# Some full matrix products of an attention-and-convolution kernel issued as one 128-column matmul instead of two 64-column ones

## The chip, the core and the metric

The kernel runs on one core of a Trainium2 chip. The time is device microseconds of one execution; a kernel's time is the median of several. Before the change it is 215.59 us, the median of three runs (215.33, 215.59 and 215.70).

The core's engines run side by side and meet at semaphores: TensorE (PE in the profile, with its weight loads shown apart as PEld), VectorE (DVE), ScalarE (ACT), GpSimd (POOL) and SyncE (SP). PE multiplies into PSUM, and ACT and DVE take the results out of it.

## The reference

Eight sequences of 576 steps with 8 heads of width 64. Linear attention without a softmax, a norm per head, and then a gated long convolution:

```python
kv  = einsum('bhsd,bhse->bhde', k, v)
out = einsum('bhsd,bhde->bhse', q, kv)
x   = out / sqrt(mean(out*out, -1) + 1e-6) * g_norm      # -> (8, 576, 512)
proj = x @ w_proj                                        # 512 -> 3 * 512
x1, x2, x3 = proj[..., :512], proj[..., 512:1024], proj[..., 1024:]
x2_conv = irfft(rfft(x2, axis=1) * rfft(filter_fft, axis=0))
out = (x1 * x2_conv * x3) @ w_out
```

## The kernel before

**The order of the work is written by hand.** The string `ORDER` at the top lists some 700 words such as `Ga1.2`: a step and the sequence that it works on. The loop at the end of the kernel runs through the words and calls each step's function, so every engine gets its instructions in exactly this order. Nothing is moved by a scheduler.

**The steps that run on PE**, and what each reads:

- `K` (L374): `kv` of one sequence, 48 small matmuls of 64 moving columns, for pairs of heads side by side. `T0`, `T1` (L412): 12 PE transposes each, of q. For sequences 3 to 7 the step `Qt` has SP issue a DMA transpose of q instead (L399).
- `O01`, `O23` (L451): q times kv, in 64x64 pieces. `R0` to `R3` (L462, or L464 through `mm2`): the sum of squares of a head, by a product with the matrix of ones `ind`.
- `Ga0` to `Ga3`, `Gb0` to `Gb3` (L637): the projections x1 and x3, 8 full products of 288 columns each; `GaP`, `GaQ`, `GbP`, `GbQ` are parts of the last of them. `rrM`, `rrT`, `abM`, `abT`: the projection x2, folded for the transform.
- `F0`, `F1`, `F2` and the remainders `F1t`, `F2t`: the forward transform as products with tables. `I01`, `Io01`, `I23`, `Io23` and the uncut forms `J..`: the inverse one. DVE and POOL multiply by the filter between them (`M..`, `A..`, tiles `tpw` and `Y`).
- `U0`, `U2`, `U4` and, for the last sequence, `V0` to `V3`: the product with `w_out`, of 512 columns.
- ACT and DVE evict: `eK` copies kv into `kvblk` (ACT, L380), `eTs` the transposed q (ACT, L416), `sq`, `ob`, `rs` and `x1..` are further ACT steps, `g..` is DVE's product of the two gates (L645), `M2` (L627) is DVE's product for `F2`.

**Three tilings of PE's array are in use.** A matmul of 128 rows and 64 weight columns uses half of the array, one of 64 rows and 64 columns a quarter, and a transpose the whole. The function `mm2` makes a full product of 128 weight columns out of two half-array matmuls, the first on columns 0 to 63 and the second on 64 to 127, with the same moving data:

```python
for c in (0, 64):
    nc.tensor.matmul(out[c:min(c + 64, m)], lhsT[:, c:min(c + 64, m)], rhs, start=start, stop=stop, tile_position=(0, c))
```

All the steps with full products call `mm2`: R, H (the filter's tables), rrM, abM, abT, F0, F1, Ga, Gb, I, J, U and V. `K`, `rrT`, `F2`, `Ff` and the idle products of `W` are in half tiles by their nature, `O`, `F1t` and `F2t` in quarter tiles, `T` and `Tb` in full ones. 2,989 matmuls run on PE in all; 1,117 full products by `mm2` are 2,234 of them.

PSUM is four tiles of two banks (`ps`), which `take` and `free` hand round: a step on PE waits until the eviction of the step that had the tile before is done.

Of the kernel before, what the change touches and what calls it, by code (L numbers as in the profile page):

```python
# [19 lines left out]
ORDER = """Lf.0 Zi.0 Z.0 W.3.2 Zt.0 An.0 W.0.12 Act.0 Zg.0 Gc.0 W.1.3 Zd.0 Zf.0 Tb1.0 Lvb.0 Lkb.0 Zz.0 Ff2.0 Ff1.0 Tb0.0 Lqb.0  # L20
# [37 lines left out]
def kernel(  # L58
# [11 lines left out]
    nc = tc.nc  # L70
# [25 lines left out]
    def take(key, n=2):  # L96
        i = min((x for x in range(4) if seen[x] is not None), key=lambda x: seen[x])
        held[key], seen[i] = i, None
        t = pair[i] if n == 2 else pair[i][:, 0]
        for _ in range(tmp.pop("idle", 0)):  # L100
            mm2(pair[i][:, 0], ind, kvblk[1].rearrange("p a b c -> p (a b c)"), start=True, stop=True)
        return t
# [5 lines left out]
    def mm2(out, lhsT, rhs, start, stop):  # L108
        mode[0] = 128
        m = lhsT.shape[-1]  # L110
        for c in (0, 64):
            nc.tensor.matmul(out[c:min(c + 64, m)], lhsT[:, c:min(c + 64, m)], rhs, start=start, stop=stop, tile_position=(0, c))  # L112

    made = {}
    mode = [128]

    def buf(name, i, shape, dt=BF16, tag=None, bufs=1):
        if (name, i) not in made:
            made[name, i] = work.tile(shape, dt, name=name, tag=tag or "%s%d" % (name, i), bufs=bufs)
        return made[name, i]  # L120
# [206 lines left out]
    def gen_h(g):  # L327
        ff = tmp['ff']
        hp = take("h")
        n = N1 if g == 0 else P  # L330
        for ri in range(2):
            for a in range(3):
                mm2(hp[:n, ri], FW[:, a, 2 * g + ri, 0:n], ff[:, a, ri], start=(a == 0), stop=(a == 2))
        u = work.tile([P, 2, DM], FP32, name="hu", tag="ot%d" % g)
        if g < 2:
            todo = [(HH[:n, g, 1], 0, cf[:n, 0, g:g + 1], cf[:n, 1, g:g + 1]),
                    (HH[:n, g, 0], 1, cf[:n, 0, g:g + 1], cf[:n, 2, g:g + 1])]
        else:
            todo = [(HM[:, i], 0, pc[:, 2 * i:2 * i + 1], pc[:, 2 * i + 1:2 * i + 2]) for i in range(2)]
        if g < 2:  # L340
            act.activation(out=u[:n], in_=hp[:n], func=AF.Copy, scale=todo[0][2])
        else:
            for i in range(2):
                act.activation(out=u[:n, i], in_=hp[:n, 0], func=AF.Copy, scale=todo[i][2])
        for i, (o_, ri, c1, c2) in enumerate(todo):
            vec.scalar_tensor_tensor(out=o_, in0=hp[:n, 1 - ri], scalar=c2, in1=u[:n, i], op0=ALU.mult, op1=ALU.add)  # L346
        free("h")
# [107 lines left out]
    def R(b, j):  # L455
        split = mode[0] == 64
        r2 = tmp['r', b, j] = take(("r", b, j))
        for h in range(2):
            x_ = sq()[:, j, h * TH:(h + 1) * TH]
            if split:  # L460
                for c in (lo, hi):
                    nc.tensor.matmul(r2[c, h, 0:TH], ind[c, c], x_[c], start=True, stop=True)  # L462
            else:
                mm2(r2[:, h, 0:TH], ind, x_, start=True, stop=True)  # L464
# [226 lines left out]
    full = [False]  # L691
# [142 lines left out]
            for e, q_ in (("s", nc.sync), ("g", nc.gpsimd), ("a", nc.scalar)):  # L834
                step["d%s%d%d" % (e, c, i)] = lambda b, c=c, i=i, q_=q_: o_dma(b, 1 + 2 * c, ot_tile(b, c // 2 * 2)[:, c % 2], (q_,), (i,))

    for word in ORDER.split():
        n, b, *idle = word.split(".")
        b, tmp["idle"] = int(b), int(idle[0]) if idle else 0
        clock[0] += 1  # L840
        step[n](b)
# [30 lines left out]
```

## Time and profile before

| | |
|---|---|
| time, median of 3 runs | 215.59 us (215.33 to 215.70) |
| profiled execution, its own time | 216.72 us |
| its span, from the first to the last instruction | 214.9 us |
| mean granted TensorE clock | 0.991 |
| PE busy | 201.8 us, 94% of the span, 2,989 matmuls |
| DVE busy | 174.9 us, 81% |
| ACT busy | 155.3 us, 72% |
| POOL busy | 59.3 us, 28% |

A row of the timeline view has the start of a group of instructions, the time until the last of them ends, the engine, the line, the operation with what it writes and reads, and the count; in brackets stands the idle time of the engine before it and who ended it. A matmul's row gives rows x weight columns, and after it the moving data. The time of one matmul contains its latency (a half-array matmul of 288 columns takes 291 ns in the mean), while the next can start long before it ends: how fast PE goes is read from start to start, not from the mean of one.

### The profile page before, as it was taken

The page shows a single profiled execution, that of the slowest core. Times are in us where ns is not written, and L with a number is a line of the kernel's source. Part 1 is how long each engine was busy: PE and PEld are TensorE (multiplying, and loading weights), DVE is VectorE, ACT ScalarE, POOL GpSimd, SP SyncE. Part 2 cuts the span into 40 slices and gives each one's busy share as a digit, 9 for nine tenths or more (in the row PEclk, how much of TensorE's full clock was granted, in tenths as well). Part 3 has the DMA queues.
Part 4 walks back from the last instruction along what each step waited for, and adds up shares of the span by engine and source line. Part 5 has one row for each costly group of instructions (what it writes and reads, how often), then busy time and mean ns, then how long its engine had stood idle before and what let it go on. Part 6 is the DMA issues. An engine that isn't in the chain of part 4 may idle for free.

```text
span 214.9 us, 6961 instructions
## 1 busy us (share of the span) xinstructions
PE 201.8 (94%) x2989; PEld 143.3 (67%) x2989; DVE 174.9 (81%) x242; ACT 155.3 (72%) x249; POOL 59.3 (28%) x88
## 2 busy tenths in 40 slices
PE   7998779999979999999999999999999999999990
PEld 6464468577858687677675868675676774697560
DVE  6565887599984999999979999798987999995650
ACT  3787777989787998897989985794865655426320
POOL 7970390036005900400063013003102100400752
PEclk9999978999999999999999999999999999999999
DMA  4999999999998999958849956231441244151573
GB/s 64 181 204 202 205 175 200 204 191 160 190 181 138 133 203 205 203 92 118 161 100 154 241 85 89 67 97 37 111 107 34 71 118 112 47 126 26 153 219 119
DMA packets 39938, 29.68 MB, mean 138 GB/s; under 512 B 14500, under 2 KB 35556, under 8 KB 39908
## 3 DMA queue, kind: packets, MB, share of 16 engines
q0 software_dynamic: 22080, 17.89, 53.6%
q1 hardware_dynamic: 17588, 11.02, 23.9%
q8 instruction: 23, 0.38, 0.8%
q10 hardware_dynamic: 240, 0.33, 0.5%
q14 instruction: 7, 0.06, 0.1%
HBM read 33.69 MB, written 9.44 MB: 201 GB/s over the span
## 4 chain that ended last, share of the span: by engine, by line
PE 83%; DMA 5%; POOL 3%; ACT 2%; DVE 2%; issue 2%; POOLq 0%; ACTq 0%; DVEq 0%
PE ps L112 73%; DMA vb<-in_v_dram 5%; PE ps L374 2%; PE ps L451 2%; PE ps L540 2%; PE ps L604 1%; PE ps L578 1%; PE ps L598 1%; DMA out_dram<-x 1%; DVE HM L346 1%; DVE HH L346 1%; POOL qb L129 1%; POOL kb L129 1%; PE ps L412 1%; ACT rstd L478 1%
## 5 line engine op out<-in xcount | busy, mean ns | idle before, releaser
L112 PE MATMUL ps<-x,wp 128*64 128x288 bf16 (+2 forms) x1024 | 73.0, 290 | 0.7 <-DVE x L492 0.6
L112 PEld LDWEIGHTS <-wp 128*64 128x64 bf16 x1024 | 59.3, 111 | 9.5 <-issue 2.7
L618 POOL TENSOR_TENSOR Y<-tpw 97x1024 bf16<-97x1024 f32 x8 | 18.9, 2364 | 109.5 <-DVE tpw L612 69.1
L612 DVE TENSOR_TENSOR tpw<-ps,HH 97x2048 f32<-97x2048 f32 (+1 forms) x16 | 36.6, 2287 | 1.8 <-PE ps L112 0.9
L112 PE MATMUL ps<-wo,yg 128*64 128x512 bf16 (+1 forms) x296 | 34.7, 374 | 0.0
L645 DVE TENSOR_TENSOR g<-ps,x 128x576 bf16<-128x576 f32 x30 | 22.5, 755 | 10.6 <-PE ps L112 9.4
L478 ACT ACTIVATE rstd<-ps,bias_eps 128x576 bf16<-128x576 f32 x32 | 23.0, 748 | 5.2 <-PE ps L112 3.8
L557 ACT CAST x<-ps 128x1024 bf16<-128x1024 f32 (+1 forms) x24 | 21.0, 879 | 7.7 <-PE ps L540 5.4
L112 PEld LDWEIGHTS <-yg 128*64 128x64 bf16 x296 | 16.3, 110 | 14.3 <-issue 1.8
L643 ACT CAST x<-ps 128x576 bf16<-128x576 f32 x30 | 19.5, 650 | 8.1 <-PE ps L112 7.8
L705 ACT CAST eo<-ps 128x576 bf16<-128x576 f32 x32 | 19.9, 658 | 6.3 <-PE ps L112 6.1
L112 PE MATMUL ps<-wp,ab 128*64 128x512 bf16 x192 | 23.3, 379 | 0.0
L467 ACT ACTIVATE sq<-ps 128x576 bf16<-128x576 f32 x32 | 20.4, 653 | 2.2 <-PE ps L451 2.0
L474 ACT ACTIVATE o<-ps,g_col 128x576 bf16<-128x576 f32 x28 | 20.6, 748 | 0.0
L112 PE MATMUL ps<-IV,Y 128*64 128x192 bf16 (+3 forms) x384 | 18.6, 239 | 1.5 <-issue 1.5
L112 PEld LDWEIGHTS <-Y 128*64 128x64 bf16 (+1 forms) x384 | 16.6, 110 | 3.4 <-issue 1.6
L788 ACT COPY ot<-ps 128x1024 f32<-128x1024 f32 x12 | 12.2, 1017 | 8.9 <-PE ps L112 8.8
L112 PEld LDWEIGHTS <-ind 128*64 128x64 bf16 x158 | 11.2, 119 | 8.5 <-DVE HH L346 1.8
L112 PEld LDWEIGHTS <-ab 128*64 128x64 bf16 x192 | 10.4, 110 | 7.7 <-issue 0.3
L492 DVE TENSOR_TENSOR x<-o,rstd 128x1152 bf16<-128x1152 bf16 x16 | 11.6, 752 | 4.7 <-ACT rstd L478 4.6
L112 PE MATMUL ps<-sq,ind 128*64 128x288 bf16 x116 | 11.0, 287 | 2.2 <-DVE HH L346 1.0
L627 DVE TENSOR_TENSOR Y<-ps,HM 128x1024 bf16<-128x1024 f32 x8 | 9.8, 1222 | 3.4 <-PE ps L604 3.1
(141 smaller groups left out, 288.7 us busy)
## 6 DMA issues: line engine op xcount, KB each, us to landing
out_dram<-ot SPq DMA_DIRECT2D x108, 64.0 KB, 1.7
vb<-in_v_dram POOLq DMA_DIRECT2D x7, 576.0 KB, 11.7
kb<-in_k_dram POOLq DMA_DIRECT2D x7, 576.0 KB, 10.7
qb<-in_q_dram POOLq DMA_DIRECT2D x7, 576.0 KB, 13.5
wp<-in_moe_w_proj_dram POOLq DMA_DIRECT2D x3, 512.0 KB, 15.5
fn<-in_moe_filter_fft_dram POOLq DMA_DIRECT2D x1, 576.0 KB, 6.5
vb<-in_v_dram POOLq DMA_DIRECT2D x2, 288.0 KB, 7.3
kb<-in_k_dram POOLq DMA_DIRECT2D x2, 288.0 KB, 6.8
```

The lines of the kernel that those rows point to most:

```text
L112: nc.tensor.matmul(out[c:min(c + 64, m)], lhsT[:, c:min(c + 64, m)], rhs, start=start, stop=stop, tile_position=(0, c))
L467: act.activation(out=halves(sq()[:, j]), in_=tmp['o', b, j][:, :, 0:TH], func=AF.Square)
L474: act.activation(out=by_time(osb(), j), in_=i_, func=AF.Copy, scale=g_col)
L478: act.activation(out=by_time(rstd(), j), in_=by_row(tmp['r', b, j]), func=AF.Abs_reciprocal_sqrt, scale=1.0 / D, bias=bias_eps)
L492: vec.tensor_mul(out=xt(b)[:, j0:j1], in0=osb()[:, j0:j1], in1=rstd()[:, j0:j1])
L557: act.copy(out=o_(), in_=tmp[key, b])
L612: vec.tensor_mul(out=t_[:n], in0=xp[:n].unsqueeze(1).to_broadcast([n, 2, 2, DM]), in1=two)
L618: op(out=Yt()[:n, 2 * g:2 * g + 2], in0=t_[:n, ::-1, 0], in1=t_[:n, ::-1, 1])
L643: act.copy(out=x1, in_=pp[:, :, 0:TH])
L645: vec.tensor_mul(out=halves(g13t(b)[:, dc]), in0=pp[:, :, 0:TH], in1=x1)
L705: act.copy(out=eo()[:, h, d0:d0 + 2], in_=tmp['i', b, d0, h][:, :, 0:TH])
L788: act.copy(out=ot, in_=tmp['u', b, c0])
```

## The change

`mm2` gets a second way: where the flag `wide[0]` is set it issues one matmul with all 128 weight columns in place of the two halves. The flag is set per word of `ORDER` by a small pass ahead of the kernel's body. The pass walks through the words, calls the tiling of each step "quarter", "half", "full" or "any" (a step made of `mm2` products can be either half or full), and collects runs of "any" steps. A run becomes full where neither neighbour is half, or where one neighbour is full; the other runs stay as they were. The order of the words is kept, and with it the order of the work on every other engine.

```diff
     def mm2(out, lhsT, rhs, start, stop):
         mode[0] = 128
         m = lhsT.shape[-1]
+        if wide[0]:
+            nc.tensor.matmul(out, lhsT, rhs, start=start, stop=stop)
+            return
         for c in (0, 64):
             nc.tensor.matmul(out[c:min(c + 64, m)], lhsT[:, c:min(c + 64, m)], rhs, start=start, stop=stop, tile_position=(0, c))
...
+    wide = [False]
+    words = ORDER.split()
+
+    def tile_of(n, last):
+        if n in ("O01", "O23", "F1t", "F2t") or n[0] == "R" and last == "quarter":
+            return "quarter"
+        if n in ("K", "Ka", "Kb", "rrT", "F2", "W") or n[:2] == "Ff":
+            return "half"
+        if n in ("T0", "T1", "Tb0", "Tb1", "Tb2", "Gc"):
+            return "full"
+        if n[0] in "RHIJUV" and n[1] != "N" or n[:2] in ("rr", "Ga", "Gb", "F0", "F1") or n in ("abM", "abT"):
+            return "any"
+        return None
+
+    runs, last = [], "half"
...
+    whole = set()
+    for a_, at, b_ in runs:
+        if (a_ != "half") + (b_ != "half") == 2 or "full" in (a_, b_):
+            whole.update(at)
...
-    for word in ORDER.split():
+    for i_, word in enumerate(words):
         n, b, *idle = word.split(".")
+        wide[0] = i_ in whole
```

Eleven runs with 334 of the 1,117 full products become full, and PE has 2,655 matmuls instead of 2,989. In the order of the program:

| run | products | before it | behind it |
|---|---|---|---|
| R0.0 | 2 | full (T1.1) | full (T0.1) |
| Ga1.0 Ga0.0 | 16 | quarter | quarter |
| R1.1 abM.0 | 10 | half (rrT.0) | full (T0.2) |
| F0.0 | 3 | full (T0.2) | full (T1.2) |
| Ga3.0 | 8 | full (T1.2) | half (K.2) |
| Gb2.0 F1.0 | 10 | quarter | quarter |
| Gb2.1 Ga0.2 F1.1 | 18 | quarter | quarter |
| Gb0.2 to F1.2 | 41 | quarter | quarter |
| U2.0 to Ga2.3 | 30 | quarter | quarter |
| Gb3.3 to abT.4 | 24 | quarter | quarter |
| U0.5 to the end | 172 | quarter (F1t.7) | the end |

PE's list, between the transposes of sequence 2 and the step F0.0 (tables FW and FX, 97 rows of result), before:

```order
L412 MATMUL ps_69<-ident,qb_74 128x96
L112 LDWEIGHTS FW
L112 MATMUL ps_68<-x_703,FW 64x512
L112 LDWEIGHTS FW
L112 MATMUL ps_68<-x_703,FW 33x512
L112 LDWEIGHTS FX
L112 MATMUL ps_68<-x_703,FX 64x512
L112 LDWEIGHTS FX
L112 MATMUL ps_68<-x_703,FX 33x512
```

And the same place now, down to the next transposes:

```order
L446 MATMUL ps_69<-ident,qb_74 128x96
L112 LDWEIGHTS FW
L112 MATMUL ps_68<-x_685,FW 97x512
L112 LDWEIGHTS FX
L112 MATMUL ps_68<-x_685,FX 97x512
L112 LDWEIGHTS FX
L112 MATMUL ps_68<-x_685,FX 97x512
L446 LDWEIGHTS qb_74
L446 MATMUL ps_67<-ident,qb_74 128x96
```

Six matmuls have become three, and the array's tiling no longer changes on the way from the transposes into F0.0 and back. Counted over the whole list, the tiling changes 60 times where it changed 64 times: twice less around F0.0 and twice less around R0.0. At R1.1 and Ga3.0 a change of tiling moves from one end of the run to the other.

The second place is row 1,717 of PE's list, in the step Io01.0 (products of Y with the table IV, 192 and 96 columns), before, with the row in the middle of these:

```order
L112 LDWEIGHTS Y
L112 MATMUL ps_66<-IV,Y 64x192
L112 LDWEIGHTS Y
L112 MATMUL ps_66<-IV,Y 64x96
L112 LDWEIGHTS Y
L112 MATMUL ps_66<-IV,Y 64x96
L112 LDWEIGHTS wp
```

Row 1,717 of the list now, again in the middle, lies in the step I01.0, which comes three steps later:

```order
L115 LDWEIGHTS Y
L115 MATMUL ps_66<-IV,Y 64x192
L115 LDWEIGHTS Y
L115 MATMUL ps_66<-IV,Y 64x192
L115 LDWEIGHTS Y
L115 MATMUL ps_66<-IV,Y 64x96
L115 LDWEIGHTS Y
```

Ahead of it 49 products have become full, so 98 rows (49 weight loads and 49 matmuls) are gone from the list, and every later instruction stands 98 rows further forward.

The third place is the start of the last run, where the quarter-tile step F1t.7 hands over to U0.5 (tiles yg and wo), before:

```order
L578 LDWEIGHTS FZ
L578 MATMUL ps_66<-x_703,FZ 64x512
L112 LDWEIGHTS yg
L112 MATMUL ps_69<-wo,yg 64x512
L112 LDWEIGHTS yg
```

And now:

```order
L612 LDWEIGHTS FZ
L612 MATMUL ps_66<-x_685,FZ 64x512
L112 LDWEIGHTS yg
L112 MATMUL ps_69<-wo,yg 128x512
L112 LDWEIGHTS yg
```

The tiling still changes once here, from quarter to full instead of from quarter to half, and from here to the end all products are full ones.

More of the change, by code (lines that the diff above doesn't have):

```diff
@@ L115 @@
     mode = [128]
+    wide = [False]
[12 more added lines that the diff above has]
+    for i_, word in enumerate(words):
+        n_ = word.split(".")[0]
+        k_ = tile_of(n_, last)
+        if k_ is None:
+            continue
+        if k_ == "any":
+            if last != "any":
+                runs.append([last, [], "quarter"])
+            runs[-1][1].append(i_)
+        elif last == "any":
+            runs[-1][2] = k_
+        last = k_
+    whole = set()
+    for a_, at, b_ in runs:
+        if (a_ != "half") + (b_ != "half") == 2 or "full" in (a_, b_):
+            whole.update(at)
     def buf(name, i, shape, dt=BF16, tag=None, bufs=1):
@@ L835 @@
                 step["d%s%d%d" % (e, c, i)] = lambda b, c=c, i=i, q_=q_: o_dma(b, 1 + 2 * c, ot_tile(b, c // 2 * 2)[:, c % 2], (q_,), (i,))
-    for word in ORDER.split():
+    for i_, word in enumerate(words):
         n, b, *idle = word.split(".")
+        wide[0] = i_ in whole
         b, tmp["idle"] = int(b), int(idle[0]) if idle else 0
```

## The prediction

> **What bounds the kernel.** First the page: the span, the busy shares, the chain that ended last, and the queue that brings PE its instructions.
>
> ```profile
> span 214.9 us, 6961 instructions
> PE 201.8 (94%) x2989; PEld 143.3 (67%) x2989; DVE 174.9 (81%) x242; ACT 155.3 (72%) x249; POOL 59.3 (28%) x88
> PE 83%; DMA 5%; POOL 3%; ACT 2%; DVE 2%; issue 2%; POOLq 0%; ACTq 0%; DVEq 0%
> q8 instruction: 23, 0.38, 0.8%
> ```
>
> PE is the bound: 83% of the chain are its matmuls. So the question is what a full product costs PE in each form. In the timeline of a steady stretch, four gates of 8 products of 288 columns, all as half-tile pairs:
>
> ```profile
> 186.08 4.09 PE L112 MATMUL ps<-x,wp 128*64 128x288 bf16 x64
> 190.00 1.16 PE L112 MATMUL ps<-IV,Y 128*64 128x288 bf16 x16
> ```
>
> 32 pairs take 190.00 - 186.08 = 3.92 us, 122.5 ns each, 0.425 ns per column. The two halves of a pair run side by side, and their weight loads cost nothing to be seen. **A full product can gain only where this stream is interrupted.** The interruptions are in the timeline around F0.0 (transposes at L412, then F0.0, transposes, Ga3.0, K.2); two grouped rows, one of PE and one of its loads, give the duration of one transpose and of its load.
>
> ```profile
> 41.73 0.38 PE L112 MATMUL ps<-wp,ab 128*64 128x512 bf16 x2
> 42.05 0.68 PE L412 MATMUL ps<-ident,qb 96*128 96x96 bf16 x12
> 42.66 0.40 PE L112 MATMUL ps<-x,FW 96*64 96x512 bf16 x2
> 42.89 0.60 PE L112 MATMUL ps<-x,FX 128*33 128x512 bf16 x4
> 43.43 0.69 PE L412 MATMUL ps<-ident,qb 96*128 96x96 bf16 x12
> 44.05 1.17 PE L112 MATMUL ps<-x,wp 128*64 128x288 bf16 x16
> 45.05 0.32 PE L374 MATMUL ps<-vb,kb 96*64 96x64 bf16 x10
> ```
>
> ```profile
> L412 PE MATMUL ps<-ident,qb 96*128 96x96 bf16 x72 | 4.1, 207 | 0.0
> L412 PEld LDWEIGHTS <-qb 96*128 96x128 bf16 x72 | 3.3, 98 | 1.1 <-issue 1.0
> ```
>
> The 12 transposes last 0.68 us and the last one 0.207, so they start (0.68 - 0.207)/11 = 43 ns apart. The last starts at 42.52, and F0.0 follows 0.14 later: the change of tiling costs 0.14 - 0.04 = 0.10 us. At 42.05 it is the same (0.32 after the last 512-column pair, which takes 0.22 at 0.425 ns per column), at 43.43 (last pair at 42.89 + 0.22 = 43.11, 0.32 again) and at 44.05 (0.14). **Each change of tiling costs PE 0.10 us, whichever two tilings.** Ga3.0 then takes 45.05 - 44.05 = 1.00 us for 8 pairs where 0.98 would do: 0.02 more for the first pair behind a change.
>
> **The steady cost of a full product.** No plain full-array product is in the trace; the nearest rows are the transposes, which are full-array matmuls with a load of 128 new weight columns each. They start 43 ns apart at 96 columns, where 0.425 x 96 is 41. So the load hides under only 41 ns of streaming, and 120 ns or more should cover it better. Bounds: 0 to 2 ns per product, up to 334 x 2 = 0.7 us in all; I take 0, since 288 columns give three times the cover. Below 0 it can't go, because the pairs already run at the column rate.
>
> The Trainium skill, "TensorE: Matmul & The Clock Gate", under "What overlaps and what doesn't", says that a weight load overlaps running matmuls only when the row groups differ. It speaks against the change, as all row groups of a full product are the same. The transposes disagree: a load of 98 ns in the mean sits in steps of 43. By the rule the loads of full products would be exposed; that is a rival below.
>
> **Changes of tiling.** There are four fewer. Two are at R0.0, in this piece of the timeline:
>
> ```profile
> 28.01 0.44 PE L112 MATMUL ps<-sq,ind 128*64 128x288 bf16 x4 [0.73 <-DVE HM L346]
> 28.38 0.68 PE L412 MATMUL ps<-ident,qb 96*128 96x96 bf16 x12
> 29.26 0.76 DVE L492 TENSOR_TENSOR x<-o,rstd 128x1152 bf16<-128x1152 bf16 x1 [0.64 <-ACT rstd L478]
> 30.07 0.64 PE L112 MATMUL ps<-x,wp 128*64 128x288 bf16 x3 [0.64 <-DVE x L492]
> ```
>
> R0.0 waits for DVE anyway, which hides the change ahead of it. The one behind it only brings T0.1 forward, and the next step that decides, Ga1.0 at 30.07, waits for DVE's x. R0.0's second product may come 0.01 sooner. I count 0 for both.
>
> The other two are around F0.0 and stand on PE's path: 2 x 0.10, and 0.02 for its second pair. At R1.1 and abM.0 one change moves ahead of the run: R1.1 starts 0.10 later, abM.0 ends where it did. At Ga3.0 one moves behind it, for another 0.02. So K.2 starts about 0.25 us sooner. Not all of it goes on; here are ACT's timeline and the step O01.2 behind K.2's eviction (`kvblk`):
>
> ```profile
> 41.07 2.10 ACT L557 CAST x<-ps 128x1024 bf16<-128x1024 f32 x2
> 43.07 2.20 ACT L416 COPY qT<-ps 128x1152 bf16<-128x1152 bf16 x2
> 45.26 0.64 ACT L643 CAST x<-ps 128x576 bf16<-128x576 f32 x1
> 46.02 1.14 ACT L380 CAST kvblk<-ps 128x256 bf16<-128x256 f32 x3
> ```
>
> ```profile
> 47.21 0.44 PE L451 MATMUL ps<-qT,kvblk 64*64 64x288 bf16 x8
> ```
>
> ACT works without a gap from 41.07 to 45.90, is free for 0.12, and evicts K.2 until 47.16; O01.2 starts 0.05 behind that. So about 0.12 can go through. Bounds: 0.02 (if the 0.10 that R1.1 loses delays ACT's row as well) and 0.25; I take **0.15**.
>
> **The instruction stall.** PE's largest single gap after 31 us waits for no semaphore. The timeline, and PE's matmuls counted up to three points:
>
> ```profile
> 61.55 0.55 PE L112 MATMUL ps<-IV,Y 128*64 128x192 bf16 x10
> 63.58 0.23 PE L112 MATMUL ps<-IV,Y 97*64 97x96 bf16 x2 [1.48 <-issue]
> 63.62 0.81 PE L112 MATMUL ps<-x,wp 128*64 128x288 bf16 x10
> ```
>
> ```profile
> 0.00:57.90 57.90, 52.13 (x727) 0.97 1.18 179
> 0.00:61.90 61.90, 56.13 (x859) 0.97 1.18 180
> ```
>
> It stops in the middle of Io01.0, ten matmuls in, 1.64 us behind the time that the two left would have started (61.94). My reading: PE ran out of instructions. Queue q8 moved 23 packets, and PE had 2 x 2,989 = 5,978 loads and matmuls, 260 to a packet. Between 57.9 and 61.9 PE used 2 x (859 - 727) = 264 of them, a whole packet in 4.0 us, where the mean is 214.9/23 = 9.3, since K.4 and K.3 pack 48 matmuls into 0.76 us each. The DMA view of 61.0 to 62.3 has one such packet, on engines that are full of loads:
>
> ```profile
> q8 instruction: 1, 0.02, 4.9%
> ```
>
> Now 98 instructions ahead of this point are gone, so the packet's edges move 98 rows on. One falls from 57.9 (start of K.4) to about 59.3, in abM.1. The other falls from row 1,717 into I01.0, second half of this timeline row:
>
> ```profile
> 65.58 1.04 PE L112 MATMUL ps<-IV,Y 128*64 128x192 bf16 x24
> ```
>
> That is near 66.1, or 64.5 without the stall. So the packet lasts 64.5 - 59.3 = 5.2 us instead of 4.0, and the stall should shrink from 1.64 by about 1.2, to 0.4. Bounds: 0 (the edge isn't there, or the request is late by as much) and 1.64. What is late next is a DMA transpose. Rows of the tile qT, its first transpose with the time to landing, and the step that reads it, O23.3:
>
> ```profile
> L399 SPq DMA_TRANSPOSE qT<-qb x1: 3554/3554/3554, 60.4 to 60.4; - x1
> DMA to landing us min/median/max: 6.9/6.9/6.9
> ```
>
> ```profile
> 67.75 0.64 PE L451 MATMUL ps<-qT,kvblk 64*64 64x288 bf16 x8
> ```
>
> It is issued at 60.44 (behind q's load, not behind PE) and lands near 67.35, so O23.3 can't start before about 67.40: at this point PE is at most 0.35 us ahead, whether it gained 0.4 or 1.3 before. Behind it stand Gb2.1 and Ga0.2, 16 pairs, and then F1.1:
>
> ```profile
> 68.33 2.38 PE L112 MATMUL ps<-x,wp 128*64 128x288 bf16 x32
> 70.52 0.41 PE L112 MATMUL ps<-x,FW 128*64 128x512 bf16 x2
> ```
>
> They take 2.19 us where 16 x 0.1225 + 0.02 = 1.98 would do: 0.21 of waiting for PSUM tiles, one of them F2.1's. F2.1 stands ahead of O23.3 and does come early, and DVE's product for it too; I let half of this wait go, 0.10. Together **0.45**, with the 0.15 contained in it.
>
> **The rest.** Six of the seven runs behind quarter tiles still have both changes, the last run only the one ahead of it. Their second product comes sooner, by 0.01 if a full load leaves 0.01 where a pair leaves 0.02 (the transposes: 11 steps of 0.0425 fill 0.47 of the 0.473). Five of these runs lie behind 67.75: **0.05**, between 0 and 0.10. The last run is half of all full products, on PE's path, with no gap to win:
>
> ```profile
> 182.60:207.20 24.60, 24.59 (x325) 18.32 (x324) 18.25 (x24) 10.59 (x15) 7.84 (x12) 1.00 0.41 106
> ```
>
> **Sum.** 0.45 + 0.05 = 0.50 us off the profiled execution, whose span is 214.9 and own time 216.72; the same amount off the median of 215.59 gives **215.1 us**.
>
> **Rivals.**
>
> *The stall stays*, because the edge falls elsewhere or the packet arrives as late as the new need. Then 0.15 + 0.05 = 0.20: 215.4. For it: I infer the packets' edges from one stall. Chance 0.26.
>
> *The transposed q lands earlier too*, and all of the stall's 1.2 goes through with 0.15 and 0.05: 214.2. Against it: the DMA engines are full there, and the transpose's issue waits for a load. Chance 0.09.
>
> *Slower: PE runs dry at another place.* The edges move behind every run, and this decides where a packet is used up faster than one is brought. The stalled packet took from 57.9 to 63.58, 5.7 us, to be replaced. The next dense stretch has K.6:
>
> ```profile
> 94.37 0.41 PE L112 MATMUL ps<-sq,ind 128*64 128x288 bf16 x4
> 96.49 0.95 PE L374 MATMUL ps<-vb,kb 96*64 96x64 bf16 x48
> 99.53 1.05 PE L112 MATMUL ps<-x,wp 128*64 128x288 bf16 x14
> ```
>
> By the shifted count a packet would last there from R3.4 (94.4) to Ga1.3 (100.0), 5.6 us, right at the limit if DMA is as full. A stall like the old one, 1.5 us, less 0.50, gives 216.6. Chance 0.09.
>
> *Slower: loads of full products show.* From 0.50/334 = 1.5 ns per product on it eats the gain. At 10 ns it costs 3.3 less 0.50: 218.4. With a whole load of 98 ns exposed it is 334 x 0.098 = 32.7: 248. This last is what the skill's rule would give; the transposes speak against both. Chance 0.06, nearly all of it near 218.
>
> **Numbers.** The forecast has 0.50. A measurement here tells about 0.2% (0.43 us) from no change, so faster means below 215.16. Of the forecast's 0.50, spread some 0.2 to either side, 0.30 is faster and 0.20 the same; the earlier landing adds 0.09 to faster and the staying stall 0.02. Faster 0.41, same 0.44, slower 0.15 (the last two rivals). The range leaves out the exposed loads and half of the earlier landing: 214.5 to 216.7.
>
> **What would show it.** Right: starts in the last run stay 122 to 123 ns apart at 288 columns; F0.0 follows the transposes without 0.10; the gap near 62 shrinks to about 0.4; O23.3 waits for qT. Wrong: starts over 124 ns apart in full runs; an "issue" gap of a microsecond anywhere, near 100 above all; a gap of 1.6 near 62 still.

## The result, and the profile after

| | before | after |
|---|---|---|
| time, median | 215.59 us (214.64 to 218.70, 22 runs) | 214.11 us (213.21 to 216.27, 22 runs) |
| profiled execution, its own time | 216.72 us | 213.90 us |
| its span | 214.9 us | 212.1 us |
| mean granted TensorE clock | 0.991 | 0.993 |

The ratio after to before is **0.9938, with a 95% interval of 0.9917 to 0.9958**: 1.3 us faster, 0.9 to 1.8. (All ratios here leave out executions more than 1.5% above the fastest of their kernel; the medians contain them.) The forecast was 215.1 with a range from 214.5: the gain is well over the 0.5 us forecast, and 214.11 lies below the range. It is near what the faster rival gave (214.2, chance 0.09).

The page of the profile after has the bound, the chain and the queue of instructions, and a group of the full products with that of their loads:

```profile
span 212.1 us, 6284 instructions
PE 197.6 (93%) x2646; PEld 136.6 (64%) x2655; DVE 174.6 (82%) x242; ACT 154.8 (73%) x249; POOL 59.3 (28%) x88
PE 78%; DMA 6%; DVE 5%; ACT 3%; issue 3%; POOL 2%; POOLq 0%; DVEq 0%
q8 instruction: 21, 0.34, 0.6%
L112 PE MATMUL ps<-x,wp 128*128 128x288 bf16 (+2 forms) x192 | 26.1, 285 | 0.8 <-DVE x L526 0.7
L112 PEld LDWEIGHTS <-wp 128*128 128x128 bf16 x192 | 18.3, 98 | 7.4 <-issue 2.2
```

PE is still the bound, and fetches 21 packets of instructions instead of 23. (Nine matmul records are missing; the 2,655 loads are complete.)

The timeline of PE after, at the four places of the prediction: F0.0 between the transposes, K.2, the former stall with O23.3 behind it, and the tail.

```profile
39.98 0.68 PE L446 MATMUL ps<-ident,qb 96*128 96x96 bf16 x12
40.49 0.38 PE L112 MATMUL ps<-x,FW 96*97 96x512 bf16 x1
40.72 0.60 PE L112 MATMUL ps<-x,FX 128*97 128x512 bf16 x2
41.15 0.67 PE L446 MATMUL ps<-ident,qb 96*128 96x96 bf16 x12
41.66 1.15 PE L112 MATMUL ps<-x,wp 128*128 128x288 bf16 x8
43.74 0.95 PE L408 MATMUL ps<-vb,kb 96*64 96x64 bf16 x48 [0.93 <-DMA vb<-in_v_dram]
...
60.22 0.61 PE L115 MATMUL ps<-IV,Y 128*64 128x192 bf16 x12
60.65 2.15 PE L115 MATMUL ps<-x,wp 128*64 128x288 bf16 x32
62.61 1.03 PE L115 MATMUL ps<-IV,Y 128*64 128x192 bf16 x24
...
64.78 0.64 PE L485 MATMUL ps<-qT,kvblk 64*64 64x288 bf16 x8
65.35 2.35 PE L112 MATMUL ps<-x,wp 128*128 128x288 bf16 x16
67.54 0.38 PE L112 MATMUL ps<-x,FW 128*128 128x512 bf16 x1
...
183.01 4.08 PE L112 MATMUL ps<-x,wp 128*128 128x288 bf16 x32
186.93 3.13 PE L112 MATMUL ps<-IV,Y 128*128 128x288 bf16 x24
```

F0.0 now follows 0.51 us behind the start of the transposes where it was 0.61. The row of Io01.0 at 60.22 has all its 12 matmuls, and the gate follows 0.43 behind: **the stall is gone to the last**, where 0.4 of it should have stayed. O23.3 at 64.78 waits for nothing, because the transposed q landed sooner after its issue (58.26) than before:

```profile
L433 SPq DMA_TRANSPOSE qT<-qb x1: 3805/3805/3805, 58.3 to 58.3; - x1
DMA to landing us min/median/max: 5.4/5.4/5.4
```

**Where the two profiles part.** Start of the same step in both, in us, from the timelines (before's rows stand in the prediction, but for O01.1's, which is below):

| step | before | after | after less before |
|---|---|---|---|
| Ga1.0 | 30.07 | 29.62 | -0.45 |
| O01.1 | 33.75 | 31.68 | -2.07 |
| T0.2 | 42.05 | 39.98 | -2.07 |
| Ga3.0 | 44.05 | 41.66 | -2.39 |
| K.2 | 45.05 | 43.74 | -1.31 |
| Ga0.1, behind Io01.0 | 63.62 | 60.65 | -2.97 |
| O23.3 | 67.75 | 64.78 | -2.97 |
| four gates in the tail | 186.08 | 183.01 | -3.07 |

The 2.8 us between the two spans are not the effect. Between Ga1.0 and O01.1 before's execution ran at half clock. Here is that stretch by windows (its length, then PE, its loads, DVE, ACT and POOL busy, then the granted clock, and the DMA engines' share and GB/s):

```profile
29.97:33.38 3.41, 3.31 (x28) 3.12 (x29) 3.27 (x10) 2.65 (x5) 2.68 (x4) 0.50 1.12 164
```

And the 16 products of Ga1.0 and Ga0.0 in both timelines of PE, before and then after:

```profile
30.07 3.75 PE L112 MATMUL ps<-x,wp 128*64 128x288 bf16 x32 [0.64 <-DVE x L492]
33.75 0.44 PE L451 MATMUL ps<-qT,kvblk 64*64 64x288 bf16 x8
```

```profile
29.62 2.12 PE L112 MATMUL ps<-x,wp 128*128 128x288 bf16 x16 [0.74 <-DVE x L526]
31.68 0.44 PE L485 MATMUL ps<-qT,kvblk 64*64 64x288 bf16 x8
```

That is 3.68 against 2.06 us, 1.62 of the difference. Another 1.08 comes back at K.2, which waits for the load of v in this execution. What the change does is in the remaining steps: -0.32 between T0.2 and Ga3.0, -1.66 at the stall, -0.10 from there to the tail. The 0.32 goes into that wait for v, so that 1.76 us are left in this pair of profiles, where the ratio gives 1.3, 0.9 to 1.8.

### The profile page after: what moved, and what is told of

The parts are those of the page before. It is cut to its first block, busy times and chain, and to the rows that moved or that the text cites. A ratio compares the mean times of both kernels' runs of the same rounds, so it can differ in the third digit from the quotient of the medians.

```text
span 212.1 us, 6284 instructions
## 1 busy us (share of the span) xinstructions
PE 197.6 (93%) x2646; PEld 136.6 (64%) x2655; DVE 174.6 (82%) x242; ACT 154.8 (73%) x249; POOL 59.3 (28%) x88
## 4 chain that ended last, share of the span: by engine, by line
PE 78%; DMA 6%; DVE 5%; ACT 3%; issue 3%; POOL 2%; POOLq 0%; DVEq 0%
PE ps L115 47%; PE ps L112 19%; DMA vb<-in_v_dram 6%; PE ps L408 3%; PE ps L485 2%; PE ps L574 1%; PE ps L353 1%; DVE HH L380 1%; PE ps L638 1%; PE ps L612 1%; PE ps L632 1%; DVE ang L248 1%; ACT IV L252 1%; DVE Y L661 1%; PE ps L306 1%
## 5 line engine op out<-in xcount | busy, mean ns | idle before, releaser
L115 PE MATMUL ps<-x,wp 128*64 128x288 bf16 (+1 forms) x640 | 45.0, 286 | 0.0
L115 PEld LDWEIGHTS <-wp 128*64 128x64 bf16 x640 | 36.5, 110 | 4.7 <-issue 0.7
L112 PE MATMUL ps<-x,wp 128*128 128x288 bf16 (+2 forms) x192 | 26.1, 285 | 0.8 <-DVE x L526 0.7
L112 PEld LDWEIGHTS <-wp 128*128 128x128 bf16 x192 | 18.3, 98 | 7.4 <-issue 2.2
L115 PE MATMUL ps<-wp,ab 128*64 128x512 bf16 x168 | 20.4, 379 | 0.0
L115 PE MATMUL ps<-wo,yg 128*64 128x512 bf16 x160 | 19.0, 380 | 0.0
L112 PE MATMUL ps<-wo,yg 128*128 128x512 bf16 (+1 forms) x64 | 14.8, 366 | 0.6 <-DVE yg L767 0.2
L115 PEld LDWEIGHTS <-ind 128*64 128x64 bf16 x142 | 9.9, 115 | 7.0 <-DVE HH L380 1.8
L115 PE MATMUL ps<-IV,Y 128*64 128x192 bf16 (+1 forms) x300 | 13.7, 233 | 0.0
L115 PEld LDWEIGHTS <-yg 128*64 128x64 bf16 x160 | 8.6, 110 | 7.8 <-issue 1.2
```

What stands on the lines that cost most here:

```text
L112: nc.tensor.matmul(out, lhsT, rhs, start=start, stop=stop)
```

## The experiments

Four theories. **S, the stall**: PE's list is fetched in packets of 256 rows (a matmul and its weight load are two rows); the change gains by moving the packets' edges, and any edit that moves them alike gains alike. **P, the products**: full products are cheaper for PE than pairs. **C, the clock**: fewer matmuls keep the clock from halving near 30 us. Later **L, the landing**: how soon the transposed q lands decides how much of the stall's 1.6 us goes through; its rival N has another cause.

Rows can be added without adding work: the idle products of `W.0.12` and `W.1.3`, at the start of the program, are cut into narrower pieces.

### Four kernels that part the theories

**e1_half_shift**: the kernel before, every product still a pair, with 156 more rows ahead (98 rows fewer and 158 more are the same place in a packet of 256):

```diff
-        for _ in range(tmp.pop("idle", 0)):
-            mm2(pair[i][:, 0], ind, kvblk[1].rearrange("p a b c -> p (a b c)"), start=True, stop=True)
+        for k_ in range(tmp.pop("idle", 0)):
+            cut = 4 if tmp["w"] == "0" else 2 if tmp["w"] == "1" else 1
+            for c0 in range(0, 512, 512 // cut):
+                cs = slice(c0, c0 + 512 // cut)
+                mm2(pair[i][:, 0, cs], ind, kvblk[1].rearrange("p a b c -> p (a b c)")[:, cs], start=True, stop=True)
...
+        tmp["w"] = b if n == "W" else ""
```

> The kernel before, all products in half tiles; the 12 idle products of W.0.12 are cut into four of 128 columns each and the 3 of W.1.3 into two, so PE's list has 156 more rows ahead of everything else and streams the same columns. 156 rows forward is 256 less 100, so the edges of the instruction packets fall where the change puts them (98 rows back) to within 2 rows. Theory S (the gain is the instruction stall near 62 us, which the shorter list moves out of the dense stretch): the gap in Io01.0 is gone or under 0.5 us, and the time is 1.0 to 1.6 us under the kernel before. Theory P (full products are themselves cheaper, or their changes of tiling are): no gain, within 0.3 us of before, and the gap of 1.5 us still there. Theory C (the clock: full products keep it up near 30 us): no gain either.

**e2_full_unshift**: the changed kernel with 96 rows added in the same way, so that the edges fall back to 2 rows from where they were:

```diff
+            cut = 4 if tmp["w"] == "0" and k_ < 8 else 1
```

> The changed kernel with 96 rows put back: 8 of the 12 idle products of W.0.12 are cut into four of 128 columns. All 334 full products stay, but the packets' edges are back at their old place in Io01.0. Theory S: the gap near 60 us is back (1 to 1.7 us) and the time is 0.2 to 0.4 us under the kernel before (what the four changes of tiling are worth). Theory P and theory C: as fast as the changed kernel, 1.0 to 1.6 us under before.

**e3_late_only**: the 285 full products behind Io01.0 alone, so no edge ahead of it moves:

```diff
     for a_, at, b_ in runs:
+        if at[0] < words.index("Io01.0"):
+            continue
```

> Full products only in the runs behind Io01.0 (Gb2.1 and later, 285 of the 334); the first 49 stay half-tile pairs, so no row ahead of Io01.0 is gone. Theory S: the gap near 62 us stays, the time is within 0.2 us of before (0.05 to 0.1 less). Theory P by products: 285/334 of the gain, 1.1 us less. Theory C: no gain, as Ga1.0 and Ga0.0 are pairs again.

**e4_early_only**: the 49 full products ahead of Io01.0 alone (the same lines with `>`).

> Full products only in the six runs ahead of Io01.0 (49 of the 334), among them all four places where a change of tiling goes or moves. Theory S: the gap is gone and the whole gain is there, 1.0 to 1.6 us less than before. Theory P by products: 49/334 of it, 0.2 us; by changes of tiling: up to 0.5 us. Theory C: the whole gain, and no half-clock stretch near 30 us.

Measured, beside the kernel before (215.48 us):

| kernel | full products | stall in Io01.0, in its profile | median | ratio, 95% interval |
|---|---|---|---|---|
| e1_half_shift | 0 | gone | 214.44 | 0.9951 (0.9920 to 0.9983) |
| e2_full_unshift | 334 | back | 215.18 | 0.9989 (0.9961 to 1.0018) |
| e3_late_only | 285 | stays | 215.74 | 1.0007 (0.9977 to 1.0037) |
| e4_early_only | 49 | gone | 214.24 | 0.9953 (0.9919 to 0.9986) |

Time follows the stall, whatever the products are. The intervals of single kernels overlap (e1's and e2's), but e1 and e4 together, whose executions have a mean of 214.4 us without those that the ratios leave out, lie 0.9 us below e2 and e3 together, 215.3, with a 95% interval (by resampling them) of 0.5 to 1.4. The timelines of e2, where it is back, and of e1, where it is gone:

```profile
60.94 0.59 PE L118 MATMUL ps<-IV,Y 128*64 128x192 bf16 x11
63.06 0.20 PE L118 MATMUL ps<-IV,Y 97*64 97x96 bf16 x1 [1.54 <-issue]
```

```profile
59.97 0.59 PE L115 MATMUL ps<-IV,Y 128*64 128x192 bf16 x12
60.40 2.13 PE L115 MATMUL ps<-x,wp 128*64 128x288 bf16 x32
```

In the kernel before, PE stopped behind the tenth matmul of Io01.0. In e2 it stops behind the eleventh: its list is 2 rows shorter up to there, and the stall has moved by just one matmul and its load. So the stall sits at a row of the list and not at a piece of work.

That it is the fetch of the list shows in the queue q8. By the DMA view in windows of 0.02 us, a packet of q8 starts at 61.10 in the profile before, and PE goes on at 63.58, 2.48 us later. In the profiles of e2, e3, e5, e8 and e12, which have the stall too, it is 2.46, 2.41, 2.29, 2.44 and 2.39, while the wait itself is from 0.93 to 1.87 us long. The end of the stall keeps its distance from the packet, and S holds.

P falls with e3: 285 full products cost what 285 pairs did, within 0.4%. C falls with e8 below, the kernel before again, which ran the same stretch with pairs at a granted clock of 1.00 (29.9 to 33.3 us), and with e4's profile, which ran the full products of Ga1.0 and Ga0.0 at half clock; its window of that stretch and its timeline:

```profile
29.70:33.10 3.40, 3.40 (x15) 2.14 (x15) 3.30 (x9) 2.38 (x4) 2.54 (x4) 0.50 1.16 182
```

```profile
29.63 3.79 PE L112 MATMUL ps<-x,wp 128*128 128x288 bf16 x16 [0.74 <-DVE x L528]
```

### Other positions

One execution each, all on one chip with the kernel before (e8). e5, e6 and e7 are the kernel before with 256, 136 and 172 rows added; the line of e1's edit that differs, in this order:

```diff
+            cut = (8 if k_ < 7 else 4) if tmp["w"] == "0" else 1
+            cut = (4 if k_ < 11 else 2) if tmp["w"] == "0" else 1
+            cut = (8 if k_ < 1 else 4) if tmp["w"] == "0" else 2 if tmp["w"] == "1" else 1
```

> The kernel before with 256 more rows ahead of everything else (idle products of W.0.12 cut into eight or four pieces). Theory S with packets of 256 rows: every edge falls where it did in the kernel before, so the gap stands again in Io01.0, 1.4 to 1.9 us. Rival, that any added rows or the longer warm-up are what removed the gap in e1_half_shift: no gap.

> The kernel before with 136 more rows in the idle products. Theory S: the packet that is used up fastest now lasts about 4.5 us by the timeline of before (3.96 there at the old edges, 5.2 at those of the change) and its end falls at the end of I01.0 or the start of Ga2.1, so a gap of 0.5 to 1.1 us stands there, five steps behind the old place, and none in Io01.0. Rival: no gap, as in e1_half_shift.

> The kernel before with 172 more rows in the idle products. Theory S: the fastest packet lasts 5.5 us, more than with the change's edges, so no gap over 0.2 us anywhere between 50 and 70 us. Rival, that the gap belongs to the place in the program and not to the packets: the gap is in Io01.0.

> The kernel before, unchanged, for a second look. Theory S: the gap in Io01.0 is 1.4 to 1.9 us again. The transposed q of sequence 3, which took 6.9 us to land in the first look and was taken for a limit at O23.3, lands in 5.1 to 7.0 us if that time varies from run to run, and in 6.9 again if it belongs to the kernel.

The single times were 214.22 (e5), 214.74 (e6), 214.73 (e7) and 215.78 us (e8); another execution of the kernel before on that chip took 215.0, so they tell little by themselves. With a whole packet of rows added the stall is again behind the tenth matmul, as in e8; here are both timelines, e5 and then e8:

```profile
59.87 0.55 PE L115 MATMUL ps<-IV,Y 128*64 128x192 bf16 x10
61.35 0.23 PE L115 MATMUL ps<-IV,Y 97*64 97x96 bf16 x2 [0.93 <-issue]
```

```profile
61.09 0.55 PE L112 MATMUL ps<-IV,Y 128*64 128x192 bf16 x10
62.90 0.23 PE L112 MATMUL ps<-IV,Y 97*64 97x96 bf16 x2 [1.27 <-issue]
```

The place was foretold, the size was not: 0.9 us of waiting in one execution, 1.3 in the other. In e6 and e7 the stall in Io01.0 was gone, as expected. The stall of 0.5 to 1.1 us that e6's expectation had at the end of I01.0 did not come: that is a miss. What came was the cap of the prediction, a wait of O23.3 for its q, 0.89 us in e6 and 0.49 in e7, where no gap over 0.2 had been expected. O23.3 in e6's timeline, and behind it the time from the issue of its q to the landing:

```profile
64.60 0.40 PE L607 MATMUL ps<-x,FZ 64*64 64x512 bf16 x2
65.89 0.44 PE L454 MATMUL ps<-qT,kvblk 64*64 64x288 bf16 x8 [0.89 <-DMA qT<-qb]
```

```profile
DMA to landing us min/median/max: 7.3/7.3/7.3
```

So the cap exists. Whether it binds depends on a landing time that was 5.3 us in e1, e2 and e4 and 5.4 after, but 6.9 before, 7.0 in e3 and 6.9 to 7.4 in e5 to e8.

### Is the landing what limits the gain?

**e9_gate_ahead**: the changed kernel with one gate moved ahead of F2.1, which puts O23.3 about 1 us later on PE. **e10_after_again**: the changed kernel once more.

```diff
-es01.0 g0.1 x12.1 F2.1 F2t.1 M2.1 Qt.3 O23.3 Gb2.1 g2.1 sq2.3
+es01.0 g0.1 x12.1 Gb2.1 g2.1 F2.1 F2t.1 M2.1 Qt.3 O23.3 sq2.3
```

> The changed kernel with Gb2.1 and g2.1 moved ahead of F2.1 in the order, so that O23.3 comes about 1 us (8 products of 0.1225 us) later on PE and the transposed q has that much more time to land. Same work, same rows up to Ga2.1. If the landing of the transposed q (5.3 us after its issue in some runs, 6.9 to 7.4 in others) is a limit of the changed kernel in part of its executions, this kernel is 0.1 to 0.8 us faster than e10 and its O23.3 never waits for qT. If the landing is late only in executions that are slow for other reasons, or F2.1's product being 1 us later is missed by DVE, it is within 0.3 us of e10. Against before: ratio 0.990 to 0.995.

> The changed kernel once more, unchanged, as the yardstick of e9 on the same chip: ratio 0.993 to 0.995 against before, no gap of PE in Io01.0, and at O23.3 either no wait (landing 5.3 us after issue) or one up to 1.3 us (landing 7 us).

**e11_after_no_q** and **e12_before_no_q** take the wait out of the changed kernel and of the kernel before; **e13_after_third** is the changed kernel beside them.

```diff
             for hp in range(2):
+                q_ = qT(b)[:, 6 * j + 3 * hp:6 * j + 3 * hp + 3]
+                if b == 3 and j > 1:
+                    q_ = wp[:, j, 288 * hp:288 * hp + 288].rearrange("p (c t) -> p c t", c=3)
                 nc.tensor.matmul(op[64 * hp:64 * hp + 64, r, 0:TH], kvblk[b % 2][64 * r:64 * r + 64, r ^ hp, j],
-                                 qT(b)[64 * r:64 * r + 64, 6 * j + 3 * hp:6 * j + 3 * hp + 3].rearrange("p c (m t) -> p m c t", m=3),
+                                 q_[64 * r:64 * r + 64].rearrange("p c (m t) -> p m c t", m=3),
                                  start=True, stop=True)
```

> The changed kernel, with O23.3 reading 288 columns of the w_proj table where it read the transposed q of sequence 3 (the output of that sequence's heads 4 to 7 is then another one); the transposes are issued as before. O23.3 can't wait for a landing any more. If the late landing of the transposed q is what gave the gain back in the last set (theory L): 0.6 to 1.6 us faster than before on any chip (ratio 0.9925 to 0.997), no gap of PE over 0.7 us between 59 and 68 us, and faster than e13 by up to 1 us where e13's q lands 7 us after its issue. If something else makes the gain differ from set to set (rival N): the same as e13 within 0.3 us, whatever e13's landing.

> The kernel before with the same edit of O23.3. Its stall of 1.5 us in Io01.0 lies ahead of O23.3 and stays, and O23.3 starts near 67 us, when the transposed q has landed or nearly. Theory L: within 0.4 us of before (ratio 0.998 to 1.001), and 0.8 to 1.6 us behind e11. Rival N, in the form that the read of qT costs something besides the wait: faster than before by as much as e11 is faster than e13.

> The changed kernel unchanged, on the chip of e11 and e12. Theory L: ratio 0.993 to 0.995 if its profile shows the transposed q landing about 5.4 us after the issue and O23.3 not waiting for it; 0.997 to 0.999 if it shows 7 us or more and a wait of 0.9 to 1.7. Rival N: no connection between the two.

| kernel | median (before beside it) | ratio, 95% interval | landing of q in its profile | wait at O23.3 |
|---|---|---|---|---|
| after, the result | 214.11 (215.59) | 0.9938 (0.9917 to 0.9958) | 5.4 | none |
| e10_after_again | 215.19 (215.36) | 0.9985 (0.9957 to 1.0013) | 7.6 | 1.72 |
| e13_after_third | 215.02 (215.46) | 0.9961 (0.9927 to 0.9995) | 7.1 | 1.40 |
| e9_gate_ahead | 214.98 (215.36) | 0.9996 (0.9968 to 1.0024) | 5.3 | none |
| e11_after_no_q | 214.32 (215.46) | 0.9953 (0.9922 to 0.9985) | 7.0 | impossible |
| e12_before_no_q | 215.44 (215.46) | 1.0010 (0.9983 to 1.0038) | 6.8 | impossible |

The changed kernel has thus been measured three times: 1.3, 0.3 and 0.8 us faster by the ratios, and e10's interval contains no change. The expectation of e10 (0.993 to 0.995) is missed. That of e13, 0.997 to 0.999 with a landing of 7 us, is missed by 0.0009, well inside the interval.

The timelines at O23.3 in e10, where all that the stall's end had gained is waited away, and in e11:

```profile
59.48 0.61 PE L115 MATMUL ps<-IV,Y 128*64 128x192 bf16 x12
59.91 2.15 PE L115 MATMUL ps<-x,wp 128*64 128x288 bf16 x32
...
64.03 0.40 PE L638 MATMUL ps<-x,FZ 64*64 64x512 bf16 x2
66.16 0.44 PE L485 MATMUL ps<-qT,kvblk 64*64 64x288 bf16 x8 [1.72 <-DMA qT<-qb]
66.53 2.13 PE L112 MATMUL ps<-x,wp 128*128 128x288 bf16 x16
68.60 0.38 PE L112 MATMUL ps<-x,FW 128*128 128x512 bf16 x1
```

```profile
66.28 0.40 PE L641 MATMUL ps<-x,FZ 64*64 64x512 bf16 x2
66.29 0.64 PE L488 MATMUL ps<-wp,kvblk 64*64 64x288 bf16 x8
```

In e10, O23.3 should have started 0.01 behind the row of FZ, as in e11, and starts 2.13 behind it. With the wait taken out, the changed kernel gains 0.47% (e11) and the kernel before gains nothing (e12), as theory L has it. Between e11 and e13 the medians differ by 0.7 us, but their intervals overlap.

The profiles show it more sharply. One stretch, from the start of Io01.0 to the four gates in the tail, leaves out the half clock near 30 us and the wait for v. Its length in each profile, from the timelines:

| profile | products | idle in the stall | wait at O23.3 | stretch |
|---|---|---|---|---|
| after, e11 | full | none | none | 122.79, 122.79 |
| e1, e4 | pairs | none | none | 122.88, 122.87 |
| before, e8, e12 | pairs | 1.48, 1.27, 1.27 | none | 124.53, 124.32, 124.32 |
| e2 | full | 1.54 | none | 124.50 |
| e5 | pairs | 0.93 | none | 123.99 |
| e6, e7 | pairs | none | 0.89, 0.49 | 123.85, 123.47 |
| e10, e13 | full | none | 1.72, 1.40 | 124.60, 124.26 |

Without stall and wait the stretch is the same to 0.1 us with full products and with pairs. The stall and the wait each lengthen it by as much as they last, to within 0.2, and with its wait e10 is as long as the kernel before. (e3 is left out for a stretch at half clock there, e9 for its other order.) So it is shown that the late landing takes the gain back in these executions. How often it is late in the executions without a profile is not known, so that it makes the whole difference between the three sets of the changed kernel is likely but not shown.

**e9 missed its expectation.** With room for q, and with no wait at O23.3 in its profile, its ratio is 0.9996 and not 0.990 to 0.995, and it is not shown to be faster than e10. Its profile shows that the moved gate costs time itself: from Io01.0 to abM.2 it takes 68.61 - 59.46 = 9.15 us where the profile after takes 68.65 - 60.22 = 8.43, with the wait for q out of both. Another loss in this profile lies at the end, where ACT took 1.14 us to issue a store that it issues in 0.32 after; the products with w_out then waited for their operand. The two rows of e9:

```profile
202.29 1.14 ACTq L793 DMA_DIRECT2D out_dram<-x  x1
205.29 1.48 PE L112 MATMUL ps<-wo,yg 128*128 128x512 bf16 x10 [0.80 <-DVE yg L767]
```

No version in this study is shown to be faster than the changed kernel.

## Why the prediction missed

- **Full products cost what pairs cost: right.** In the tail 32 of them take 186.93 - 183.01 = 3.92 us, 122.5 ns each, to the digit what 32 pairs took before. Their loads, 98 ns in the mean, hide under products of the same row groups. The Trainium skill, "TensorE: Matmul & The Clock Gate", "What overlaps and what doesn't", has the overlap only where the row groups differ. The 122.5 ns speak against that here, and the rival that rested on it (248 us) is out, as are its milder forms.
- **A change of tiling costs 0.10 us: right.** T0.2 to Ga3.0 takes 1.68 us instead of 2.00: two changes gone, 0.20, and one moved behind Ga3.0, 0.10, as the diff said. R0.0 added nothing, and Ga1.0 behind it still waits for DVE. What of the 0.25 at K.2 passes the eviction can't be seen, because K.2 waited 0.93 for v in the profile after.
- **The instruction stall: the mechanism right, the size too small.** The edges moved and the stall went, but all of its 1.64 us, not 1.2. The prediction took one packet's 5.7 us for the time of every packet. At the same position PE waited 0.93 us in e5, 1.27 in e8, 1.48 in the profile before and 1.87 in e3, and in each it went on 2.3 to 2.5 us after the packet's start. So it is the packet's start, measured against PE's work, that varies by more than the 0.4. One reading was too strong: the DMA engines, "full of loads" from 61.0 to 62.3, were so until 61.1, and loads took 45% of their time in that window.
- **The cap at O23.3: the step that failed.** "O23.3 can't start before about 67.40" took the issue at 60.44 and the landing 6.9 later from one execution and used both as constants. Both moved. Against PE's start of Io01.0 (61.55 before, 60.22 after) the issue came 0.85 us sooner (58.26), and the landing took 5.4, 1.5 less. The cap had left PE 0.35 of the stall's 1.64, so 1.29 more had to pass, and the shorter landing alone was enough for it. Over all the profiles of this study the landing takes 5.3 to 5.4, in five of them, or 6.8 to 7.6, in ten, with nothing between. With the short one the cap is no limit and the whole stall's worth goes through. With the long one the forecast's sum is near: 0.5 us forecast, 0.2 and 0.4 between the medians of e10 and e13, with one profile each. So the forecast described one of two cases, and a chance of 0.09 for the other was too low on the evidence of one trace. That the rival's 214.2 comes so near is partly luck: it counted 1.2 for the stall and 0.15 at K.2, where the two profiles have 1.64 and nothing.
- **Half of the wait behind O23.3 goes: not so after, but so in e10.** From the 16 products to F1.1 it took 2.19 us before and takes 67.54 - 65.35 = 2.19 after; in e10, where O23.3 waits, 2.07.
- **The rest, 0.05: 0.10**, within its bounds. The lead grows from 2.97 at O23.3 to 3.07 in the tail, and the stretch of the table above is 0.09 shorter after than in e1.
- **PE running dry near 100 us: did not happen.** PE has no gap over 0.7 us in the profile after behind K.2's, down to the stores.

## What to carry to other kernels

A gap that waits for no semaphore, in the middle of a step, may be the instruction fetch. Test it by adding rows with no work ahead of it: if the gap moves by as many rows, any edit ahead of it will move the time too, and the edit's own worth has to be measured at the same position in the packet. When one trace shows a DMA landing just in time, put a spread on that landing before using it as a cap, since one execution gives no spread.

## What the runs showed of the hardware

- PE's fetch goes by 256 rows: 256 rows more bring the stall back behind the same matmul (e5), and 2 rows fewer move it by one (e2); 136, 156 and 172 rows more do not bring it (e6, e1, e7), with the same work. PE goes on 2.3 to 2.5 us after the start of a packet on q8, in six profiles. The stall came in the one packet that the prediction's count has used up in 4.0 us; that so dense a stretch is needed was not varied by itself.
- The DMA transpose of one sequence's q lands in two groups of times, 5.3 to 5.4 and 6.8 to 7.6 us after its issue, and the changed kernel itself showed 5.4, 7.6 and 7.1 in three profiles. The four executions on one chip (e5 to e8) were all in the long group, but another chip showed 5.3 (e9) and 7.6 (e10), and a third 5.3 (e1, e2, e4) and 7.0 (e3). What decides between them was not found.
- A stretch of 3.4 us at half clock near 30 us stood in the profiles of the kernel before, of e4 and of e12, and one from 63.5 to 66.9 in e3's, right behind its stall; no other profile has one, that of e8, the kernel before again, included. Near 30 us it costs an execution some 1.6 us, and two single profiles with and without it differ by more than the change is worth.
